# A third weight buffer, an earlier weight load and a rearranged head loop in a decode-attention gradient kernel

## The chip, the cores and the metric

The kernel runs on one core of a Trainium2 chip. The metric is device time in microseconds (us), the median over several runs. The profiled execution of each kernel is some 2 us shorter in its span than its timed run, so spans are compared with spans and timed runs with timed runs.

Engine names in the profile: PE is TensorE's matmuls, PEld its weight loads, DVE is VectorE, ACT is ScalarE, POOL is GpSimd, SP is SyncE. In this kernel SP issues nearly all loads and POOL issues nearly all stores. The order in which each engine runs its instructions is chosen by a scheduler in the framework and is fixed when the kernel is built. I call it the built order. It is not always the order of the source.

## The reference, cut to what matters

One decode step of a block, and all its gradients: layer norm, attention against a cache, and a gated MLP, both added to the input.

```python
# D=640, 32 heads, Dh=128, Sk=8192 cached positions, F=1728, all bf16
q  = (xn @ wq) per head;   p = softmax(q @ K^T * Dh**-0.5);   o = p @ V
y  = x + o @ wo + (silu(xn @ w1) * (xn @ w3)) @ w2
# returned: y, and the gradients by x, K, V, wq, wo, w1, w3, w2
```

There is one query row, so the gradients of a head's cache are outer products: `dV = P (x) do` and `dK = U (x) q`, where `do = wo . grad_out` for that head, `U = P * (V.do - sum(P * V.do))`. Each is as large as the cache itself: 2 MB for K and 2 MB for V per head. The kernel reads 151.67 MB and writes 151.34 MB.

## The kernel before

A K or V tile of 2 MB is loaded into one of ten slots, used by TensorE, overwritten in place with its gradient by DVE, and stored from the same slot. Only then is the slot free for the next load. Four heads form a *group*. They share a slice of `wq` and one of `wo` (640 KB each), which are loaded, used, overwritten with their gradients and stored in the same manner.

```python
wpool = ctx.enter_context(tc.tile_pool(name="wp", bufs=2))    # group weights
tpool = ctx.enter_context(tc.tile_pool(name="tp", bufs=5))    # "KT": transposed K/V pieces
junk  = consts.tile([P, D], BF16, name="junk")                # one tile for thrown-away output
...
def load_group(g):                       # SP queue
    wq_g = wpool.tile([P, NC, GW], BF16, name="wq_g", tag="wq_g")      # rows of 1024 bytes
    nc.sync.dma_start(wq_g[:], wq_v[:, :, g * GW:(g + 1) * GW])
    wo_g = wpool.tile([P, GH, D], BF16, name="wo_g", tag="wo_g")       # rows of 1280 bytes
    nc.sync.dma_start(wo_g[:], wo_v[:, g * GH:(g + 1) * GH, :])
...
def prep_group(g):
    ...                                  # wide q product, on TensorE, from wq_g
    for hh in range(GH):                 # "the wo product", on DVE
        nc.vector.scalar_tensor_tensor(junk[:], wo_g[:, hh, :], 1.0, g_bc[:], ALU.mult, ALU.mult,
                                       accum_out=do_c[:, hh:hh + 1])
    ...
def phase_b(h):
    ...                                  # sums over V and K on TensorE
    for lo in range(0, J, J // 2):
        outer(Vt, doh, P2, lo, lo + J // 2)          # DVE, dV over V
    nc.gpsimd.dma_start(dvc[h], Vt[:])
    free_slots.append(Vt); load_next()               # next K or V load, into a free slot
    for lo in range(0, J, J // 2):
        outer(Kt, qh, U2, lo, lo + J // 2)           # DVE, dK over K
    nc.gpsimd.dma_start(dkc[h], Kt[:])
    free_slots.append(Kt); load_next()
...
def finish_group(g):
    ...                                  # dwo over wo_g (4 DVE instructions), store
    for ci in range(NC):                 # "the wq pairs"
        nc.vector.scalar_tensor_tensor(junk[:, 0:GW], wq_g[:, ci, :], 1.0, dqb[:], ALU.mult, ALU.mult,
                                       accum_out=dxa[:, ci, g:g + 1])
        nc.vector.tensor_scalar(wq_g[:, ci, :], dqb[:], xn_col[:, ci:ci + 1], None, ALU.mult)
    nc.gpsimd.dma_start(dwq_v[:, :, g * GW:(g + 1) * GW], wq_g[:])
...
for h in range(H):
    g, hh = divmod(h, GH)
    if hh == 2 and g + 1 < NG:
        load_group(g + 1)
    if hh == 3 and g + 1 < NG:
        prep_group(g + 1)
    phase_b(h)
    if h == 1:
        mlp()
    if h + 1 < H:
        phase_k(h + 1)                   # K.q, softmax
        phase_v(h + 1)                   # V.do
    if hh == GH - 1:
        finish_group(g)
```

## Time and profile before

| | before |
|---|---|
| time, first three runs | 802.82 us (801.28 to 804.2) |
| span of the profiled run | 796.0 us |
| moved by DMA | 304.61 MB, mean 383 GB/s |
| TensorE busy | 76% |
| VectorE busy | 56% |
| VectorE waiting for a `wo` load | 119.2 us in 6 waits |

First the page of the kernel before: busy time by engine, then the span in 40 slices (each digit is a busy share in tenths), with the mean DMA rate of each slice below.

```profile
span 796.0 us, 25112 instructions
PE 601.1 (76%) x11271; PEld 553.2 (69%) x11271; DVE 444.3 (56%) x771; ACT 327.1 (41%) x652; POOL 53.1 (7%) x93
...
PE   3988880189989549992799819995599918999981
...
DMA  8999999996999998999899998999999998998656
GB/s 328 388 425 424 423 424 428 422 373 244 415 421 426 429 381 340 412 409 418 354 379 403 426 425 324 393 404 422 376 375 408 411 426 349 374 400 363 274 212 278
DMA packets 35182, 304.61 MB, mean 383 GB/s; under 512 B 2836, under 2 KB 14036, under 8 KB 18692
```

The DMA rate tops out at 420 to 430 GB/s, and the kernel reaches that in many slices. The Trainium skill ("DMA: Bandwidth & Descriptors", Specifications) names 435 GB/s as fabric ceiling, and the trace agrees to within a few per cent. But there are dips (244, 340, 354, 324, 349 GB/s) and a slow end (274, 212, 278). TensorE's row has holes (`01`, `54`, `27`, `81`), about one per group of four heads.

The waits of the kernel before tell what stands in those holes. The columns are what waited, for what, total us, number of waits, longest wait. The first fence is of the engines:

```profile
DVE junk L231 <- DMA wo_g<-in_A_wo_dram: 119.2, 6, 31.5
...
PEld L218 <- DMA wq_g<-in_A_wq_dram: 34.3, 1, 34.3
```

The second is of SP's queue, in the same kernel:

```profile
SPq L115 <- DMA out_dram<-kv: 556.8, 56, 21.5
...
SPq L103 <- DMA out_dram<-wo_g: 48.8, 6, 18.3
SPq L101 <- DMA out_dram<-wq_g: 11.6, 6, 3.2
```

Line 231 is the wo product. Six times DVE waits for the load of the next group's `wo`, 20 us on average. SP in turn waits for the store of the old `wo` gradient (48.8 us in all) before it can issue that load: with two buffers, the load of group g+1 goes into the buffer of group g-1.

One of the six, on the timeline of DVE before (start, duration, instruction, and in brackets the idle time ahead of it with what ended it):

```profile
454.80 0.22 DVE L291 TENSOR_REDUCE mrow<-sA 128x1 f32<-128x64 f32 x1
455.04 0.17 DVE L333 MEMSET hb<- 128x129 f32 x1
472.60 0.83 DVE L231 SCALAR_TENSOR_TENSOR junk<-wo_g,g_bc 128x640 bf16<-128x640 bf16 x1 [17.39 <-DMA wo_g<-in_A_wo_dram]
...
473.35 0.29 DVE L295 TENSOR_REDUCE negM<-sA 128x1 f32<-128x128 f32 x1
```

and on the timeline of SP before:

```profile
454.72 0.38 SPq L103 DMA_DIRECT2D wo_g<-in_A_wo_dram  x1
464.60 0.33 SPq L115 DMA_DIRECT2D kv<-in_A_k_cache_dram  x1
469.85 0.33 SPq L115 DMA_DIRECT2D kv<-in_A_v_cache_dram  x1
471.94 0.38 SPq L101 DMA_DIRECT2D wq_g<-in_A_wq_dram  x1
```

DVE has computed the row maximum of a head (`mrow`) at 455.02. The next step of that softmax, `negM`, comes at 473.35, behind the first wo product. DVE runs in order, so the softmax of a head that needs nothing of this `wo` stands still for 17.39 us.

What the stall does to the DMA engines is seen in the windows of the kernel before (stretch, its length, busy us and instruction count of PE, PEld, DVE, ACT and POOL, then TensorE's granted clock, DMA share, GB/s):

```profile
465.00:470.00 5.00, 0.00 (x0) 0.00 (x0) 0.00 (x0) 0.00 (x0) 0.00 (x0) 0.50 0.97 394
480.00:485.00 5.00, 4.70 (x119) 4.57 (x116) 5.00 (x4) 1.82 (x4) 0.30 (x1) 1.00 0.50 177
740.00:760.00 20.00, 18.74 (x386) 17.54 (x386) 12.36 (x13) 9.65 (x19) 1.09 (x2) 1.00 0.52 213
```

During the stall the DMA engines still have work (394 GB/s). The price comes 10 us later, when what is queued has been moved and no slot has come free (177 GB/s), and at the end of the span, where loads are over and only stores are left (213 GB/s). The granted clock also falls to 0.50 while TensorE stands still, and is 1.00 again at 480 us. The Trainium skill ("TensorE: Matmul & The Clock Gate", Part 1) says that an idle TensorE falls to half clock after a few us; the trace agrees: TensorE's last instruction before the stall ends at 456.8 us, and the clock is halved at 461.2.

### The profile page before, as it was taken

Reading aid. Unit: us, or ns where it says so; the run is one execution under the profiler, and the core shown is the slowest. Engines: PE = TensorE matmul, PEld = TensorE weight load, DVE = VectorE, ACT = ScalarE, POOL = GpSimd, SP = SyncE. Lnnn points to the kernel's source line nnn. Section 1 sums busy time; section 2 is a strip of 40 time slices with the busy share of each in tenths; the row PEclk is TensorE's granted clock in tenths of the full one; section 3 lists DMA queues with packets and bytes.
Section 4 is the critical chain, followed back from the end, with each engine's and each line's share of the span. In section 5 each row is a group of like instructions: output and inputs, shape, how many; then the busy total and the mean of one; then the engine's idle time right before and its main releaser. Section 6 shows DMA issues by size and latency. Waiting matters only on the chain. (4 is left out here: it accounts for less than half of the span.)

```text
span 796.0 us, 25112 instructions
## 1 busy us (share of the span) xinstructions
PE 601.1 (76%) x11271; PEld 553.2 (69%) x11271; DVE 444.3 (56%) x771; ACT 327.1 (41%) x652; POOL 53.1 (7%) x93
## 2 busy tenths in 40 slices
PE   3988880189989549992799819995599918999981
PEld 2877870088888438892788818895588818888871
DVE  4479463138646436572655715575465717558567
ACT  2621540055455214552355405553155514555540
POOL 0001000000000000000000100000000000001001
PEclk9998995589999869997899959999699978999996
DMA  8999999996999998999899998999999998998656
GB/s 328 388 425 424 423 424 428 422 373 244 415 421 426 429 381 340 412 409 418 354 379 403 426 425 324 393 404 422 376 375 408 411 426 349 374 400 363 274 212 278
DMA packets 35182, 304.61 MB, mean 383 GB/s; under 512 B 2836, under 2 KB 14036, under 8 KB 18692
## 3 DMA queue, kind: packets, MB, share of 16 engines
q1 hardware_dynamic: 21828, 151.35, 47.1%
q0 software_dynamic: 12960, 151.34, 45.8%
q8 instruction: 88, 1.44, 0.7%
q10 hardware_dynamic: 288, 0.33, 0.2%
q14 instruction: 18, 0.15, 0.0%
HBM read 151.67 MB, written 151.34 MB: 381 GB/s over the span
## 5 line engine op out<-in xcount | busy, mean ns | idle before, releaser
L270 ACT COPY KT<-pT 128x512 f32<-128x512 f32 x512 | 293.8, 588 | 202.9 <-PE pT L268 162.4
L268 PE MATMUL pT<-ident_f,kv 128*128 128x128 f32 x2048 | 334.8, 287 | 0.1
L268 PEld LDWEIGHTS pT<-ident_f,kv 128*128 128x128 f32 x2048 | 230.1, 145 | 0.7 <-issue 0.3
L279 PEld LDWEIGHTS <-KT 128*128 128x128 bf16 x4096 | 182.7, 99 | 26.1 <-ACT KT L270 18.7
L316 DVE TENSOR_TENSOR kv<-do_g,P 128x4096 bf16<-128x4096 bf16 x64 | 146.3, 2286 | 31.3 <-PE hb L339 31.3
L316 DVE TENSOR_TENSOR kv<-qs_g,U 128x4096 bf16<-128x4096 bf16 x64 | 144.2, 2284 | 0.4 <-PE hb L345 0.4
L279 PE MATMUL dA<-cz,KT 128*128 128x64 bf16 x2048 | 102.4, 196 | 3.9 <-ACT KT L270 2.2
L279 PE MATMUL sA<-cz,KT 128*128 128x64 bf16 x2048 | 100.5, 193 | 3.9 <-ACT KT L270 0.3
L231 DVE SCALAR_TENSOR_TENSOR junk<-wo_g,g_bc 128x640 bf16<-128x640 bf16 x32 | 26.1, 816 | 119.3 <-DMA wo_g<-in_A_wo_dram 119.2
L345 PEld LDWEIGHTS <-kv 128*128 128x128 bf16 x2048 | 67.9, 98 | 20.8 <-issue 20.7
L299 PE MATMUL sA<-rsum,ones_f 128*128 128x1 f32 x64 | 13.3, 276 | 90.6 <-ACT E L298 87.9
L345 PE MATMUL hb<-U,kv 128*128 128x64 bf16 x2048 | 69.2, 193 | 16.1 <-DVE U L342 11.1
L299 PEld LDWEIGHTS sA<-rsum,ones_f 128*128 128x128 f32 x64 | 10.5, 207 | 97.4 <-ACT E L298 97.4
L339 PE MATMUL hb<-P,kv 128*128 128x64 bf16 x2048 | 68.3, 192 | 0.3 <-issue 0.3
L339 PEld LDWEIGHTS <-kv 128*128 128x128 bf16 x2048 | 67.8, 98 | 0.5 <-issue 0.4
L336 DVE SCALAR_TENSOR_TENSOR junk<-dA,P 128x64 f32<-128x64 f32 x32 | 7.2, 224 | 94.8 <-PE dA L279 94.7
L349 POOL DMA_DIRECT2D out_dram<-kv x32 | 17.4, 542 | 488.8 <-DVE kv L316 488.8
L298 ACT ACTIVATE E<-sA,negM 128x64 f32<-128x64 f32 x32 | 10.2, 319 | 86.3 <-DVE negM L295 86.2
L218 PE MATMUL pT<-wq_g,xn_col_bf 128*128 128x512 bf16 x40 | 13.0, 441 | 38.5 <-DMA wq_g<-in_A_wq_dram 34.2
L357 ACT COPY od_g<-hb 128x2 f32<-128x2 f32 x32 | 5.1, 160 | 85.5 <-DVE kv L316 48.1
L218 PEld LDWEIGHTS <-xn_col_bf 128*128 128x128 bf16 x40 | 3.7, 106 | 41.8 <-DMA wq_g<-in_A_wq_dram 34.3
L302 DVE RECIPROCAL rZ<-sA 128x1 f32<-128x1 f32 x32 | 5.4, 168 | 40.5 <-PE sA L299 40.5
(131 smaller groups left out, 344.1 us busy)
## 6 DMA issues: line engine op xcount, KB each, us to landing
out_dram<-kv POOLq DMA_DIRECT2D x64, 2048.0 KB, 13.8
kv<-in_A_k_cache_dram SPq DMA_DIRECT2D x32, 2048.0 KB, 13.0
kv<-in_A_v_cache_dram SPq DMA_DIRECT2D x32, 2048.0 KB, 14.6
wq_g<-in_A_wq_dram SPq DMA_DIRECT2D x8, 640.0 KB, 12.2
wo_g<-in_A_wo_dram SPq DMA_DIRECT2D x8, 640.0 KB, 16.9
out_dram<-wo_g POOLq DMA_DIRECT2D x8, 640.0 KB, 12.2
out_dram<-wq_g POOLq DMA_DIRECT2D x8, 640.0 KB, 15.6
kv<-in_B_w_dram SPq DMA_DIRECT2D x2, 1728.0 KB, 19.2
```

Of the source, the lines that this page charges most:

```text
L218: nc.tensor.matmul(ps_q[:, 0:GW], lhsT=xn_col_bf[:, ci:ci + 1].to_broadcast([P, P]), rhs=wq_g[:, ci, :], start=(ci == 0), stop=(ci == NC - 1))
L231: nc.vector.scalar_tensor_tensor(junk[:], wo_g[:, hh, :], 1.0, g_bc[:], ALU.mult, ALU.mult, accum_out=do_c[:, hh:hh + 1])
L268: nc.tensor.transpose(pT[:, k * P:(k + 1) * P], W3[:, 4 * c + k, :], ident_f[:])
L270: nc.scalar.copy(KT[:].rearrange("p k w -> p (k w)"), pT[:])
L279: nc.tensor.matmul(out_[:, 0:J], lhsT=KTb[:, k, par, :], rhs=cz[:, par, a, J - 2 - 2 * i:ZW - 2 * i], start=(i == 0 and par == 0), stop=(p ...
L298: nc.scalar.activation(E[:], sA[:, 0:J], ACTF.Exp, bias=negM[:], scale=1.0, accum_out=rsum[:])
L299: nc.tensor.matmul(sA[:, J + P:J + P + 1], lhsT=ones_f[:], rhs=rsum[:], start=False, stop=True, skip_group_check=True)
L316: nc.vector.tensor_tensor(dst[:, lo * DH:hi * DH].rearrange("p (j a b) -> p j a b", a=DH // 2, b=2), vec.rearrange("p (a b) -> p a b", b=2 ...
L336: nc.vector.scalar_tensor_tensor(junk2[:], dA[:, 0:J], 1.0, P2[:, :, 0], ALU.mult, ALU.mult, accum_out=rdot[:])
L339: nc.tensor.matmul(hb[:, 0:RW], lhsT=V3[:, j, :], rhs=P2[:, j, 0:1].to_broadcast([P, RW]), start=False, stop=(j == J - 1), skip_group_chec ...
L345: nc.tensor.matmul(hb[:, RW:2 * RW], lhsT=K3[:, j, :], rhs=U2[:, j, 0:1].to_broadcast([P, RW]), start=False, stop=(j == J - 1), skip_group ...
L349: nc.gpsimd.dma_start(dvc[h], Vt[:])
```

## The change

The intent, as given: three weight-group buffers, so that each group is loaded one head ahead of its first use without waiting for a store; and the softmax chain of head h+1 placed between the outer products of head h. To make room in memory for the third buffer, several tiles are removed or lent. The core of the diff:

```diff
-    wpool = ctx.enter_context(tc.tile_pool(name="wp", bufs=2))
-    tpool = ctx.enter_context(tc.tile_pool(name="tp", bufs=5))
+    wpool = ctx.enter_context(tc.tile_pool(name="wp", bufs=3))
+    tpool = ctx.enter_context(tc.tile_pool(name="tp", bufs=4))
 ...
 def load_next():
         kind, h = pending.pop(0)
+        if kind == "K" and h % GH == GH - 1 and h // GH + 1 < NG:
+            load_group(h // GH + 1)
 ...
-    junk = consts.tile([P, D], BF16, name="junk")
 ...
 def prep_group(g):
-        ps_q = pst()                                  # wide q product and its copy: gone
-        ...
+        junk = t_tile()[:, 0:D]                       # a KT tile, taken anew each time
         for hh in range(GH):
-            nc.vector.scalar_tensor_tensor(junk[:], wo_g[:, hh, :], 1.0, g_bc[:], ALU.mult, ALU.mult,
+            nc.vector.scalar_tensor_tensor(junk, wo_g[:, hh, :], 1.0, g_bc[:], ALU.mult, ALU.mult,
                                            accum_out=do_c[:, hh:hh + 1])
-        ps_o = pst()                                  # wide do broadcast and its copy: gone
-        ...
+    def rows(h):                                      # per head: q and do rows, two 128x128 products, one copy
+        ...
 ...
 def finish_group(g):
-        dqb = small.tile([P, GW], BF16, name="dqb", bufs=1)
+        dqb = t_tile()[:, 0:GW]
         for ci in range(NC):
-            nc.vector.scalar_tensor_tensor(junk[:, 0:GW], wq_g[:, ci, :], 1.0, dqb[:], ALU.mult, ALU.mult,
+            nc.vector.scalar_tensor_tensor(wq_g[:, ci, :], wq_g[:, ci, :], 1.0, dqb, ALU.mult, ALU.mult,
                                            accum_out=dxa[:, ci, g:g + 1])
 ...
 for h in range(H):
         g, hh = divmod(h, GH)
-        if hh == 2 and g + 1 < NG:
-            load_group(g + 1)
         if hh == GH - 1 and g + 1 < NG:
             prep_group(g + 1)
-        phase_b(h)
+        sums(h)
+        outer_v(h, 0, J // 2)
+        outer_v(h, J // 2, J)
+        store("V", h)
         if h == 1:
             mlp()
         if h + 1 < H:
-            phase_k(h + 1)
-            phase_v(h + 1)
+            rows(h + 1)
+            dots_k(h + 1)
+        outer_k(h, 0, J // 2)
+        if h + 1 < H:
+            probs(h + 1)
+        outer_k(h, J // 2, J)
+        store("K", h)
+        if h + 1 < H:
+            dots_v(h + 1)
```

More of the change, by code (lines that the diff above doesn't have):

```diff
@@ L90 @@
     RW = 64
-    x_bc_bf = consts.tile([P, D], BF16, name="x_bc_bf")
-    nc.scalar.dma_start(x_bc_bf[:], A_x.rearrange("a b d -> (a b d)").partition_broadcast(P))
+    x_kt = tpool.tile([P, 4, P], F32, name="x_kt", tag="KT")
+    x_bc_bf = x_kt[:].rearrange("p k w -> p (k w)").bitcast(BF16)[:, 0:D]
+    nc.scalar.dma_start(x_bc_bf, A_x.rearrange("a b d -> (a b d)").partition_broadcast(P))
     g_bc = consts.tile([P, D], BF16, name="g_bc")
@@ L150 @@
     nc.vector.tensor_copy(ident_bf[:], ident_f[:])
-    ones_f = consts.tile([P, P], F32, name="ones_f")
-    nc.vector.memset(ones_f[:], 1.0)
-    negones_f = consts.tile([P, P], F32, name="negones_f")
-    nc.vector.memset(negones_f[:], -1.0)
+    pm_one = consts.tile([P, 2], F32, name="pm_one")
+    nc.vector.memset(pm_one[:, 0:1], 1.0)
+    nc.vector.memset(pm_one[:, 1:2], -1.0)
+    ones_b = pm_one[:, 0:1].to_broadcast([P, P])
+    negones_b = pm_one[:, 1:2].to_broadcast([P, P])
     one_bf = consts.tile([P, 1], BF16, name="one_bf")
@@ L190, in pst @@
         return ps_t.tile([P, 512], F32, name="pT", tag="pT")
-    junk = consts.tile([P, D], BF16, name="junk")
     msum = consts.tile([P, 1], F32, name="msum")
-    nc.vector.tensor_reduce(msum[:], x_bc_bf[:], AX.X, ALU.add)
+    nc.vector.tensor_reduce(msum[:], x_bc_bf, AX.X, ALU.add)
     nc.vector.tensor_scalar(negmean[:], msum[:], -1.0 / D, None, ALU.mult)
     sumsq = consts.tile([P, 1], F32, name="sumsq")
-    nc.vector.scalar_tensor_tensor(junk[:], x_bc_bf[:], negmean[:], x_bc_bf[:], ALU.add, ALU.mult,
+    nc.vector.scalar_tensor_tensor(t_tile()[:, 0:D], x_bc_bf, negmean[:], x_bc_bf, ALU.add, ALU.mult,
                                    accum_out=sumsq[:])
@@ L215, in prep_group @@
         wq_g, wo_g = G_["wq"], G_["wo"]
-        ps_q = pst()
-        for ci in range(NC):
-            nc.tensor.matmul(ps_q[:, 0:GW], lhsT=xn_col_bf[:, ci:ci + 1].to_broadcast([P, P]), rhs=wq_g[:, ci, :],
-                             start=(ci == 0), stop=(ci == NC - 1))
-        qs_g = wpool.tile([P, GH, DH], BF16, name="qs_g", tag="qs_g")
-        nc.scalar.activation(qs_g[:].rearrange("p h d -> p (h d)"), ps_q[:, 0:GW], ACTF.Copy, scale=scale)
         cb = wpool.tile([P, 2, GH], BF16, name="cb", tag="cb")
@@ L228, in prep_group @@
         nc.scalar.activation(cb[:, 0, :], ps_c[:, 0:GH], ACTF.Copy, scale=scale)
+        junk = t_tile()[:, 0:D]
         do_c = wpool.tile([P, GH], F32, name="do_c", tag="do_c")
         for hh in range(GH):
-            nc.vector.scalar_tensor_tensor(junk[:], wo_g[:, hh, :], 1.0, g_bc[:], ALU.mult, ALU.mult,
+            nc.vector.scalar_tensor_tensor(junk, wo_g[:, hh, :], 1.0, g_bc[:], ALU.mult, ALU.mult,
                                            accum_out=do_c[:, hh:hh + 1])
         nc.vector.tensor_copy(cb[:, 1, :], do_c[:])
-        ps_o = pst()
-        for hh in range(GH):
-            nc.tensor.matmul(ps_o[:, hh * DH:(hh + 1) * DH], lhsT=cb[:, 1, hh:hh + 1].to_broadcast([P, P]),
-                             rhs=ident_bf[:], start=True, stop=True)
-        do_g = wpool.tile([P, GH, DH], BF16, name="do_g", tag="do_g")
-        nc.scalar.copy(do_g[:].rearrange("p h d -> p (h d)"), ps_o[:, 0:GW])
         ps_m = pst()
@@ L248, in prep_group @@
         od_g = wpool.tile([P, GH, 2], F32, name="od_g", tag="od_g")
-        G_.update(qs=qs_g, cm=cm_g, do=do_g, od=od_g)
+        G_.update(cb=cb, cm=cm_g, od=od_g)
     hd = {}
@@ L281, in dots, with dots_k @@
                                          start=(i == 0 and par == 0), stop=(par == 1), skip_group_check=True)
-    def phase_k(h):
+    def rows(h):
         g, hh = divmod(h, GH)
-        cm = grp[g]["cm"]
+        cb, cm = grp[g]["cb"], grp[g]["cm"]
         cz = cz_tiles[h % 2]
         nc.vector.tensor_copy(cz[:, :, :, J - 2:J], cm[:, :, :, hh, :])
+        ps_r = pst()
+        for a in range(2):
+            nc.tensor.matmul(ps_r[:, a * DH:(a + 1) * DH], lhsT=cb[:, a, hh:hh + 1].to_broadcast([P, P]),
+                             rhs=ident_bf[:], start=True, stop=True)
+        qd = small.tile([P, 2, DH], BF16, name="qd")
+        nc.scalar.copy(qd[:].rearrange("p a d -> p (a d)"), ps_r[:, 0:2 * DH])
+        hd[h] = dict(cz=cz, qd=qd)
+    def dots_k(h):
+        S_ = hd[h]
         sA = ps_s.tile([P, 512], F32, name="sA", tag="sA")
-        dots(kv_tiles[("K", h)], sA, cz, 0)
+        dots(kv_tiles[("K", h)], sA, S_["cz"], 0)
         mrow = small.tile([P, 1], F32, name="mrow")
@@ L298, in phase_k, with probs, dots_v @@
         nc.scalar.activation(E[:], sA[:, 0:J], ACTF.Exp, bias=negM[:], scale=1.0, accum_out=rsum[:])
-        nc.tensor.matmul(sA[:, J + P:J + P + 1], lhsT=ones_f[:], rhs=rsum[:],
+        nc.tensor.matmul(sA[:, J + P:J + P + 1], lhsT=ones_b, rhs=rsum[:],
                          start=False, stop=True, skip_group_check=True)
+        S_.update(sA=sA, E=E)
+    def probs(h):
+        S_ = hd[h]
         rZ = small.tile([P, 1], F32, name="rZ")
-        nc.vector.reciprocal(rZ[:], sA[:, J + P:J + P + 1])
+        nc.vector.reciprocal(rZ[:], S_["sA"][:, J + P:J + P + 1])
         P2 = small.tile([P, J, 2], BF16, name="P2")
-        nc.vector.tensor_scalar(P2[:], E[:].unsqueeze(2).to_broadcast([P, J, 2]), rZ[:], None, ALU.mult)
-        hd[h] = dict(P2=P2)
-    def phase_v(h):
-        g, hh = divmod(h, GH)
-        cz = cz_tiles[h % 2]
+        nc.vector.tensor_scalar(P2[:], S_["E"][:].unsqueeze(2).to_broadcast([P, J, 2]), rZ[:], None, ALU.mult)
+        S_["P2"] = P2
+    def dots_v(h):
+        S_ = hd[h]
         dA = ps_d.tile([P, 512], F32, name="dA", tag="dA")
-        dots(kv_tiles[("V", h)], dA, cz, 1)
-        hd[h]["dA"] = dA
+        dots(kv_tiles[("V", h)], dA, S_["cz"], 1)
+        S_["dA"] = dA
     def outer(dst, vec, pair, lo, hi):
@@ L319, in outer, with sums @@
             pair[:, lo:hi, :].unsqueeze(2).to_broadcast([P, n, DH // 2, 2]), ALU.mult)
-    def phase_b(h):
+    def sums(h):
         g, hh = divmod(h, GH)
-        G_ = grp[g]
-        qh = G_["qs"][:, hh, :]
-        doh = G_["do"][:, hh, :]
-        Kt = kv_tiles.pop(("K", h))
-        Vt = kv_tiles.pop(("V", h))
-        S_ = hd.pop(h)
+        S_ = hd[h]
         P2, dA = S_["P2"], S_["dA"]
-        V3 = Vt[:].rearrange("p (j d) -> p j d", d=DH)
-        K3 = Kt[:].rearrange("p (j d) -> p j d", d=DH)
+        V3 = kv_tiles[("V", h)][:].rearrange("p (j d) -> p j d", d=DH)
+        K3 = kv_tiles[("K", h)][:].rearrange("p (j d) -> p j d", d=DH)
@@ L332, in phase_b @@
         hb = ps_h.tile([P, 2 * RW + 1], F32, name="hb", tag="hb")
         nc.vector.memset(hb[:], 0.0)
-        junk2 = small.tile([P, J], F32, name="junk2", bufs=1)
+        U2 = small.tile([P, J, 2], BF16, name="U2")
         rdot = small.tile([P, 1], F32, name="rdot")
-        nc.vector.scalar_tensor_tensor(junk2[:], dA[:, 0:J], 1.0, P2[:, :, 0], ALU.mult, ALU.mult, accum_out=rdot[:])
-        nc.tensor.matmul(hb[:, 2 * RW:2 * RW + 1], lhsT=negones_f[:], rhs=rdot[:], start=False, stop=True, skip_group_check=True)
+        nc.vector.scalar_tensor_tensor(U2[:, :, 0], dA[:, 0:J], 1.0, P2[:, :, 0], ALU.mult, ALU.mult, accum_out=rdot[:])
@@ L338, in phase_b @@
+        nc.tensor.matmul(hb[:, 2 * RW:2 * RW + 1], lhsT=negones_b, rhs=rdot[:], start=False, stop=True,
+                         skip_group_check=True)
         for j in range(J):
-            nc.tensor.matmul(hb[:, 0:RW], lhsT=V3[:, j, :], rhs=P2[:, j, 0:1].to_broadcast([P, RW]), start=False, stop=(j == J - 1),
-                             skip_group_check=True)
-        U2 = small.tile([P, J, 2], BF16, name="U2")
-        nc.vector.scalar_tensor_tensor(U2[:], dA[:, 0:J].unsqueeze(2).to_broadcast([P, J, 2]), hb[:, 2 * RW:2 * RW + 1], P2[:],
-                                       ALU.add, ALU.mult)
@@ L344, in phase_b @@
-        for j in range(J):
-            nc.tensor.matmul(hb[:, RW:2 * RW], lhsT=K3[:, j, :], rhs=U2[:, j, 0:1].to_broadcast([P, RW]), start=False, stop=(j == J - 1),
-                             skip_group_check=True)
-        for lo in range(0, J, J // 2):
-            outer(Vt, doh, P2, lo, lo + J // 2)
-        nc.gpsimd.dma_start(dvc[h], Vt[:])
-        free_slots.append(Vt)
-        load_next()
-        for lo in range(0, J, J // 2):
-            outer(Kt, qh, U2, lo, lo + J // 2)
-        nc.gpsimd.dma_start(dkc[h], Kt[:])
@@ L355, in phase_b @@
-        free_slots.append(Kt)
-        load_next()
-        nc.scalar.copy(G_["od"][:, hh, :], hb[:, RW - 1:RW + 1])
+            nc.tensor.matmul(hb[:, 0:RW], lhsT=V3[:, j, :], rhs=P2[:, j, 0:1].to_broadcast([P, RW]), start=False,
+                             stop=(j == J - 1), skip_group_check=True)
+        nc.vector.scalar_tensor_tensor(U2[:], dA[:, 0:J].unsqueeze(2).to_broadcast([P, J, 2]),
+                                       hb[:, 2 * RW:2 * RW + 1], P2[:], ALU.add, ALU.mult)
+        for j in range(J):
+            nc.tensor.matmul(hb[:, RW:2 * RW], lhsT=K3[:, j, :], rhs=U2[:, j, 0:1].to_broadcast([P, RW]), start=False,
+                             stop=(j == J - 1), skip_group_check=True)
@@ L359, with outer_v, outer_k, store @@
+        nc.scalar.copy(grp[g]["od"][:, hh, :], hb[:, RW - 1:RW + 1])
+        S_["U2"] = U2
+    def outer_v(h, lo, hi):
+        outer(kv_tiles[("V", h)], hd[h]["qd"][:, 1, :], hd[h]["P2"], lo, hi)
+    def outer_k(h, lo, hi):
+        outer(kv_tiles[("K", h)], hd[h]["qd"][:, 0, :], hd[h]["U2"], lo, hi)
+    def store(kind, h):
+        t = kv_tiles.pop((kind, h))
+        nc.gpsimd.dma_start((dkc if kind == "K" else dvc)[h], t[:])
+        free_slots.append(t)
+        load_next()
     dxa = consts.tile([P, NC, NG], F32, name="dxa")
@@ L370, in finish_group @@
                              rhs=ident_bf[:], start=True, stop=True)
-        dqb = small.tile([P, GW], BF16, name="dqb", bufs=1)
-        nc.scalar.copy(dqb[:], ps_b[:, 0:GW])
+        dqb = t_tile()[:, 0:GW]
+        nc.scalar.copy(dqb, ps_b[:, 0:GW])
         for hh in range(GH):
@@ L380, in finish_group @@
         for ci in range(NC):
-            nc.vector.scalar_tensor_tensor(junk[:, 0:GW], wq_g[:, ci, :], 1.0, dqb[:], ALU.mult, ALU.mult,
+            nc.vector.scalar_tensor_tensor(wq_g[:, ci, :], wq_g[:, ci, :], 1.0, dqb, ALU.mult, ALU.mult,
                                            accum_out=dxa[:, ci, g:g + 1])
-            nc.vector.tensor_scalar(wq_g[:, ci, :], dqb[:], xn_col[:, ci:ci + 1], None, ALU.mult)
+            nc.vector.tensor_scalar(wq_g[:, ci, :], dqb, xn_col[:, ci:ci + 1], None, ALU.mult)
         nc.gpsimd.dma_start(dwq_v[:, :, g * GW:(g + 1) * GW], wq_g[:])
@@ L503 @@
     prep_group(0)
-    phase_k(0)
-    phase_v(0)
+    rows(0)
+    dots_k(0)
+    probs(0)
+    dots_v(0)
     for h in range(H):
         g, hh = divmod(h, GH)
-        if hh == 2 and g + 1 < NG:
-            load_group(g + 1)
-        if hh == 3 and g + 1 < NG:
+        if hh == GH - 1 and g + 1 < NG:
             prep_group(g + 1)
-        phase_b(h)
+        sums(h)
+        outer_v(h, 0, J // 2)
+        outer_v(h, J // 2, J)
+        store("V", h)
         if h == 1:
@@ L515 @@
         if h + 1 < H:
-            phase_k(h + 1)
-            phase_v(h + 1)
+            rows(h + 1)
[7 more added lines that the diff above has]
+            dots_v(h + 1)
+        hd.pop(h)
         if hh == GH - 1:
@@ L532 @@
     ps_f = pst()
-    nc.tensor.matmul(ps_f[:, 0:2], lhsT=ones_f[:], rhs=st[:], start=True, stop=True)
+    nc.tensor.matmul(ps_f[:, 0:2], lhsT=ones_b, rhs=st[:], start=True, stop=True)
     nst = consts.tile([P, 2], F32, name="nst")
```

## The prediction

> **What bounds the kernel now.** The DMA engines, and a stall at each group boundary. The page: span 796 us, 304.6 MB moved, mean 383 GB/s. Where slots turn freely (35 to 165 and 200 to 270 us in the windows view) the mean is about 420 GB/s at a DMA share of 1.0. The Trainium skill ("DMA: Bandwidth & Descriptors", Specifications) gives 435 GB/s as fabric ceiling; the trace agrees to a few per cent. At 420 the traffic takes 725 us.
>
> TensorE is not the long-run limit. Unstalled, head follows head every 17.7 us (outer products at 484.3 and 502.0 us); a head's K and V traffic is 8.39 MB, 20 us at 420 GB/s, about 21.5 with its share of the projection weights.
>
> But TensorE stands still 15 to 35 us per group boundary: in 455 to 475 us nearly unused, and DVE ends a 17.4-us wait on the wo load. The waits view sums 119 us in six such waits. The SP queue view shows why: the load waits for the store of an earlier group from the two-buffer pool (wo 48.8 us over six, wq 11.6), among cache loads. DMA meanwhile goes on at 420 GB/s; the price comes later: a dip after each restart (480 to 485 us: 177 GB/s; 180 to 185: nothing), and a tail. The last V load is issued at 705 us with four heads still to do: 740 to 780 us run at 213 to 225 GB/s.
>
> **Removed.** A third buffer takes the store out of the load's way. In the built order groups 1 and 2 are queued just before K3 and K7, later ones two heads earlier still. The boundary stalls go. TensorE loses the wide q product (40 of 0.38 us, 15 us) and gains two small products a head.
>
> **Added.** KT buffers fall from 5 to 4, also lent as scratch to group work: 0 to 5 us.
>
> **Moved.** The scheduler undoes nearly all of the softmax interleaving: in most heads max, negated max, reciprocal and P still stand after both K outer products of the preceding head. 0 to 2 us.
>
> **How much counts.** Not the 119 us of waits: DMA covers most. The DMA idle time counts: by windows (1 minus share, times length) about 28 us of dips, 25 of tail. Estimate: loads end when all but about 9.5 MB has moved: 293 MB at 420 GB/s plus 4 us start, 702 us; from V landing to the end about 30 us (as after 766 us in before): 732; weights in 1-KB rows and remaining dips about 14: span 746. Timed runs were 0.9% over the span: 753 us.
>
> Predicted **753 us**, range 738 to 785. Faster by over 2%: 0.93; within 2%: 0.06; slower: 0.01.
>
> **What would show it.** (1) No DVE wait on wo at boundaries beyond a few us. (2) SP waits on weight stores near zero. (3) Mean rate above 400 GB/s, share about 1.0 from 20 to 700 us. (4) TensorE waits become short, on K and V loads; heads 20 to 22 us apart. (5) Last V load issued no earlier than before, tail under 35 us.
>
> **What would make it wrong.** K's sums of a head stand behind the next head's K transposes on TensorE, so slots are held while waiting for loads: DMA could dip in the steady state. Or scratch in the KT pool stalls TensorE at boundaries, or the MLP, with fewer buffers, drains the DMA queue.

## The result, and the profile after

| | before | after |
|---|---|---|
| time, four runs each | 802.05 us (800.57 to 804.2) | 749.69 us (748.93 to 751.46) |
| ratio after / before | | 0.9348 (0.9318 to 0.9378) |
| span | 796.0 | 748.2 |
| mean DMA rate | 383 GB/s | 407 GB/s |
| mean granted TensorE clock | 0.901 | 0.927 |

A ratio is the mean time of one kernel's fast runs over the mean of the other's of the same rounds, so it is not quite the ratio of the medians quoted. The brackets are 95% intervals.

The page of the kernel after:

```profile
span 748.2 us, 25141 instructions
PE 594.4 (79%) x11263; PEld 550.9 (74%) x11263; DVE 445.3 (60%) x771; ACT 329.8 (44%) x668; POOL 53.6 (7%) x93
...
PE   2988798993889999429986999829989499998961
...
DMA  8999999999999999999999999999998999999976
GB/s 324 387 420 423 421 422 429 427 414 430 423 420 425 424 428 422 425 429 427 390 362 411 424 428 422 379 424 430 427 417 316 423 426 430 425 427 426 425 294 259
```

The engines do the same work in nearly the same busy time. The DMA row is full nearly throughout. What is left of dips are slices of 362, 379 and 316 GB/s, and the end.

The waits of the kernel after, for the engines:

```profile
PE pT L260 <- DMA kv<-in_A_k_cache_dram: 70.7, 7, 24.5
...
DVE KT L229 <- PE dA L271: 15.4, 7, 2.2
```

and for SP's queue:

```profile
SPq L118 <- DMA out_dram<-kv: 195.1, 21, 23.6
...
SPq L102 <- DMA out_dram<-wq_g: 14.3, 2, 7.2
...
SPq L104 <- DMA out_dram<-wo_g: 12.0, 2, 6.0
```

The wo product (now line 229) waits for no load any more, only for TensorE, 2.2 us at most. SP waits 26.3 us for weight stores in place of 60.4. In their place a new wait has come: TensorE waits seven times for a K load, 24.5 us at the longest. That one, on the timeline of TensorE after:

```profile
306.87 0.27 PE L282 MATMUL pT<-ident_bf,cb 128*128 128x128 bf16 x2
331.61 2.79 PE L260 MATMUL pT<-ident_f,kv 128*128 128x128 f32 x12 [24.46 <-DMA kv<-in_A_k_cache_dram]
```

The next such episode starts in SP's queue after:

```profile
331.56 0.38 SPq L104 DMA_DIRECT2D wo_g<-in_A_wo_dram  x1
336.43 0.38 SPq L102 DMA_DIRECT2D wq_g<-in_A_wq_dram  x1
341.32 45.67 SPq L118 DMA_DIRECT2D kv<-in_A_k_cache_dram  x1
387.16 2.95 SPq L118 DMA_DIRECT2D kv<-in_A_v_cache_dram  x1
```

The issue of one K load took 45.67 us, where others take 0.33. The next longest were 42.74, 37.10, 24.33, 21.90, 19.91 and 19.69 us. All seven are the K load right behind a pair of weight loads; the eighth (14.16 us) is the next K load after one of them. And the windows of the kernel after:

```profile
315.00:325.00 10.00, 0.00 (x0) 0.00 (x0) 0.00 (x0) 0.00 (x0) 0.58 (x1) 0.50 1.02 431
385.00:390.00 5.00, 3.46 (x107) 3.33 (x104) 4.96 (x7) 0.37 (x1) 0.00 (x0) 1.00 0.73 263
```

TensorE stands still for all of 315 to 325 us, but now the DMA engines move 431 GB/s meanwhile. A dip to 263 GB/s comes at the end of the second episode. The longest issue does not go with the longest pause: the next wait of TensorE for a K load, at 412.61 us, was 6.8 us.

### Where the time went, counted in DMA time

Both kernels move the same bytes. So the difference of their spans must be a difference of DMA rate, and the question is only where. I took the windows view in 5-us steps and added up (1 - rate / 425 GB/s) x 5 us over each stage. A step above 425 GB/s counts as nothing lost.

| stage (us) | before | scratch edits alone | after | wide packets | GpSimd queue |
|---|---|---|---|---|---|
| 0 to 20 | 4.7 | 4.6 | 4.5 | 3.6 | 4.7 |
| 20 to 120 | 2.8 | 2.7 | 2.9 | 2.7 | 3.1 |
| 120 to 700 | 47.8 | 23.1 | 15.6 | 5.2 | 7.3 |
| 700 to end | 28.2 | 25.5 | 13.1 | 20.7 | 19.3 |
| sum | 83.4 | 56.1 | 36.2 | 32.2 | 34.5 |
| span | 796.0 | 768.6 | 748.2 | 743.7 | 747.3 |

("Scratch edits alone", "wide packets" and "GpSimd queue" are experiments below; sums are of unrounded values.) From before to after the sum falls by 47.2 us, and the span by 47.8. With equal bytes the two must nearly agree, so this is arithmetic and no evidence; what the table shows is the place. Of this, 32 us came from the dips between 120 and 700 us and 15 from the end. Nothing came from the first 120 us.

### The profile page after: what moved, and what is told of

It reads as the page before. It is cut to its first block, busy times and chain, and to the rows that moved or that the text cites. A ratio compares the mean times of both kernels' runs of the same rounds, so it can differ in the third digit from the quotient of the medians.

```text
span 748.2 us, 25141 instructions
## 1 busy us (share of the span) xinstructions
PE 594.4 (79%) x11263; PEld 550.9 (74%) x11263; DVE 445.3 (60%) x771; ACT 329.8 (44%) x668; POOL 53.6 (7%) x93
## 5 line engine op out<-in xcount | busy, mean ns | idle before, releaser
L260 PE MATMUL pT<-ident_f,kv 128*128 128x128 f32 x2048 | 334.7, 287 | 75.3 <-DMA kv<-in_A_k_cache_dram 70.7
L321 DVE TENSOR_TENSOR kv<-qd,U 128x4096 bf16<-128x4096 bf16 x64 | 144.3, 2285 | 48.5 <-PE hb L345 48.5
L321 DVE TENSOR_TENSOR kv<-qd,P 128x4096 bf16<-128x4096 bf16 x64 | 145.7, 2286 | 42.1 <-PE hb L340 42.1
L345 PEld LDWEIGHTS <-kv 128*128 128x128 bf16 x2048 | 68.6, 98 | 13.2 <-issue 13.0
L345 PE MATMUL hb<-U,kv 128*128 128x64 bf16 x2048 | 69.5, 193 | 9.3 <-DVE U L342 6.4
L358 POOL DMA_DIRECT2D out_dram<-kv x64 | 34.9, 546 | 567.8 <-DVE kv L321 309.1
L336 DVE SCALAR_TENSOR_TENSOR U<-dA,P 128x64 bf16<-128x64 f32 x32 | 7.4, 231 | 77.0 <-PE dA L271 77.0
L285 ACT CAST qd<-pT 128x256 bf16<-128x256 f32 x32 | 12.0, 375 | 54.4 <-PE pT L282 54.4
L229 DVE SCALAR_TENSOR_TENSOR KT<-wo_g,g_bc 128x640 bf16<-128x640 bf16 x32 | 26.4, 824 | 15.9 <-PE dA L271 15.4
L293 DVE TENSOR_REDUCE mrow<-sA 128x1 f32<-128x64 f32 x32 | 6.5, 203 | 33.3 <-PE sA L271 33.2
L384 DVE SCALAR_TENSOR_TENSOR wq_g<-wq_g,KT 128x512 bf16<-128x512 bf16 x40 | 26.2, 686 | 0.0
L297 DVE TENSOR_REDUCE negM<-sA 128x1 f32<-128x128 f32 x32 | 9.3, 291 | 14.5 <-PE sA L294 14.5
L301 PEld LDWEIGHTS sA<-rsum,pm_one 128*128 128x128 f32 x64 | 9.5, 187 | 11.2 <-ACT E L300 11.2
```

Of the source, the lines that this page charges most:

```text
L229: nc.vector.scalar_tensor_tensor(junk, wo_g[:, hh, :], 1.0, g_bc[:], ALU.mult, ALU.mult, accum_out=do_c[:, hh:hh + 1])
L260: nc.tensor.transpose(pT[:, k * P:(k + 1) * P], W3[:, 4 * c + k, :], ident_f[:])
L285: nc.scalar.copy(qd[:].rearrange("p a d -> p (a d)"), ps_r[:, 0:2 * DH])
L297: nc.vector.tensor_reduce(negM[:], sA[:, J:J + P], AX.X, ALU.max, negate=True)
L301: nc.tensor.matmul(sA[:, J + P:J + P + 1], lhsT=ones_b, rhs=rsum[:], start=False, stop=True, skip_group_check=True)
L321: nc.vector.tensor_tensor(dst[:, lo * DH:hi * DH].rearrange("p (j a b) -> p j a b", a=DH // 2, b=2), vec.rearrange("p (a b) -> p a b", b=2 ...
```

## The experiments

The explanation that the change itself suggests, and that the prediction gave, is this: the third buffer takes the weight store out of the load's way, and so the stalls at group boundaries go. Rivals: the early load, with any number of buffers; the loop order; the per-head rows in place of the wide q product; and the edits made only to save memory.

### The loop order, undone

```diff
+        sums(h); outer_v(h, 0, J // 2); outer_v(h, J // 2, J); store("V", h)
+        outer_k(h, 0, J // 2); outer_k(h, J // 2, J); store("K", h)
+        if h == 1: mlp()
+        if h + 1 < H:
+            rows(h + 1); dots_k(h + 1); probs(h + 1); dots_v(h + 1)
```

> The changed kernel with the loop order of before: both V outer products, both K outer products, both stores, then rows, K dots, softmax and V dots of the next head. Weight buffers and load position stay changed. Theory B (third buffer): the interleaving is worth nothing, so 748 to 753 us, within 0.5% of the changed kernel (749.7). Theory I (interleaving): a good part of the 52 us is lost, 765 us or more.

Measured: 750.52 us, ratio 0.9359 (0.9327 to 0.939); the change has 0.9348. The rearranged loop is worth 0.8 us in the medians, less than the intervals can tell from nothing. In the built order of the changed kernel the interleaving survives in one head of each group only: in the other three both K outer products stand ahead of the next head's maximum, as before.

### Two buffers, or the load in its old place, or both

```diff
# e2: two buffers
-    wpool = ctx.enter_context(tc.tile_pool(name="wp", bufs=3))
+    wpool = ctx.enter_context(tc.tile_pool(name="wp", bufs=2))
# e3: the load in its old place
-        if kind == "K" and h % GH == GH - 1 and h // GH + 1 < NG:
-            load_group(h // GH + 1)
+        if hh == 2 and g + 1 < NG:          # in the head loop
+            load_group(g + 1)
# e4: both
```

> The changed kernel with two weight-group buffers instead of three; the early position of the load and the interleaving stay. Theory B: the load again waits for the store of an earlier group, at the head of the in-order load queue; TensorE stalls return, 780 to 805 us, SP waits on weight stores of 40 us or more in all. Theory I: 765 us or less.

> The changed kernel with three buffers, but the group load back at its old place in the loop (head 2 of the group before). In the built order only the load of group 1 then comes late (after V6 instead of before K3); later ones are hoisted to nearly the same places, since a buffer is free. Theory B: one long stall of TensorE at the first boundary (some 30 us near 120 to 160 us), most of it covered by DMA: 750 to 760 us. Theory P (position of the load is what matters, not the buffer): 780 us or more.

> Both undone: two buffers and the old load position; what is left of the change is the interleaving, the row products per head and four KT buffers. Theory B: nearly the time of before, 785 to 805 us. Theory I: 775 us or less.

Measured, with the ratio to the kernel before:

| | load at the old place | load one head ahead |
|---|---|---|
| two buffers | 769.89 us, 0.96 (0.9551 to 0.9648) | 761.15 us, 0.9474 (0.9424 to 0.9524) |
| three buffers | 755.68 us, 0.9425 (0.9394 to 0.9456) | 749.69 us, 0.9348 (0.9318 to 0.9378) |

Theory B missed twice here: it expected 780 to 805 us for two buffers and 785 to 805 for both undone. Yet with two buffers SP's waits for weight stores did return, as it expected:

```profile
SPq L104 <- DMA out_dram<-wo_g: 46.3, 6, 15.7
SPq L102 <- DMA out_dram<-wq_g: 42.8, 6, 7.5
```

That is 89.1 us, more than the 60.4 of the kernel before, in a kernel that is 42 us faster (761.15 against 803.59). So these waits do not set the time by themselves.

Buffers and load together take 20 us (769.89 to 749.69). The buffer is worth 11 to 14 us, the early load 6 to 9. In the kernel with three buffers and the old load place, one boundary still shows the old stall, a 31.4-us wait of the wo product on its load and a 34.1-us wait on `wq`: that of group 1, whose load in the built order comes late, behind V6.

The surprise is the upper left cell. With neither the buffer nor the early load, and with a loop order that the run above had shown to be worth nothing, the kernel was still 4% faster than before. Some 32 of the 52 us come from something else. What else had changed was the row products, one KT buffer fewer, and the edits to save memory.

### The scratch edits, alone, on the kernel before

```diff
# f3: both of these, and nothing else, on the kernel before
+        junk_ = t_tile()[:, 0:D]
-            nc.vector.scalar_tensor_tensor(junk[:], wo_g[:, hh, :], 1.0, g_bc[:], ALU.mult, ALU.mult,
+            nc.vector.scalar_tensor_tensor(junk_, wo_g[:, hh, :], 1.0, g_bc[:], ALU.mult, ALU.mult,   # f3b
-            nc.vector.scalar_tensor_tensor(junk[:, 0:GW], wq_g[:, ci, :], 1.0, dqb[:], ALU.mult, ALU.mult,
+            nc.vector.scalar_tensor_tensor(wq_g[:, ci, :], wq_g[:, ci, :], 1.0, dqb[:], ALU.mult, ALU.mult,   # f3a
```

> The kernel before with both scratch edits and nothing else: two weight buffers, the old load position, the old loop, the wide q product, five KT buffers. If the scratch edits explain why undoing the buffers and the load position gave 770 us and not 802, this gives 766 to 774 us too. If the row products, the interleaving or the slimmer group work do, it stays above 785 us.

> The kernel before with one edit: the elementwise product of the wq gradient is written back over wq instead of into the shared scratch tile. In the built order this alone lets the group's five wq pairs run before the outer products, so the wq store is queued with the wo store, and the next wq load with the wo load. The wo product of the next group stays where it was, two heads early in VectorE's in-order stream. Theory D (that early product blocks VectorE until wo lands): little changes, 790 to 802 us, VectorE still waits 80 us or more on wo. Theory W (the late wq store and the split loads are what costs): 770 to 780 us.

> The kernel before with one edit: the throw-away output of the wo product goes into a KT buffer instead of the shared scratch tile. In the built order this moves the wo product from head 4g+1 to head 4g+3, its place in the program; the wq pairs stay spread between the outer products. Theory D: the wait on wo goes (except at the first group), 770 to 785 us with two weight buffers still. Theory W: 795 to 803 us.

Measured, with the kernel before at 804.47 us:

| | time | ratio to before |
|---|---|---|
| f3a: wq pairs in place | 801.82 us | 0.9971 (0.9914 to 1.0027) |
| f3b: wo product into a KT tile | 782.59 us | 0.974 (0.9694 to 0.9786) |
| f3: both | 770.33 us | 0.9586 (0.9541 to 0.963) |

Two edits that were made to save memory take 34 us by themselves, with two buffers, the old load place, the old loop, the wide q product and five KT buffers. That is 34 us of the 52 us, and it is what the upper left cell above has (770.33 against 769.89), so what else that kernel had changed (the row products, the loop order, one KT buffer fewer) adds up to nothing that can be seen. That single effects cancel is not excluded. One edit alone is worth nothing, the other 22 us, and the two together 34: they help each other.

What changed is the built order. With the thrown-away output in another tile, the scheduler put the same instructions in another order. This is DVE's built order over one group, from the finishing of the old group to the use of the next `wo` (wo4: gradient of `wo`; dx and wq: the wq pairs; dc: the wo product for the next group; OV, OK: outer products; each `|` starts a head):

```
before  rdot wo4 dx OV wq dx U2 wq dx OV wq dx OK wq dx OK wq | mrow dc negM dc rZ dc P dc rdot OV U2 OV OK2 | ... | ...
f3a     rdot wo4 dx2 wq2 dx2 wq2 dx U2 wq OV2 OK2             | mrow dc negM dc rZ dc P dc rdot OV U2 OV OK2 | ... | ...
f3b     rdot wo4 dx OV wq dx U2 wq dx OV wq dx OK wq dx OK wq | mrow negM rZ P rdot OV U2 OV OK2 | ... | mrow negM rZ P dc2 rdot dc2 OV ...
f3      rdot wo4 dx2 wq2 dx2 wq2 dx U2 wq OV2 OK2             | mrow negM rZ P rdot OV U2 OV OK2 | ... | mrow negM rZ P dc2 rdot dc2 OV ...
```

The f3b edit moves the wo product by two heads, from the second head of a group to the fourth, where the source has it, and out of the middle of a softmax. The f3a edit finishes the wq pairs before the outer products, so that the store of the old `wq` is issued sooner and SP can load the next `wq` sooner: in the same group the `wq` load is issued 17.2 us after the `wo` load before, 17.4 in f3b, but 6.4 in f3a and 7.6 in f3, with no K or V load between. The waits follow. Of f3a:

```profile
DVE junk L231 <- DMA wo_g<-in_A_wo_dram: 121.1, 6, 28.7
```

of f3b:

```profile
PEld L218 <- DMA wq_g<-in_A_wq_dram: 96.1, 6, 33.7
...
DVE KT L232 <- DMA wo_g<-in_A_wo_dram: 31.0, 1, 31.0
```

and of f3:

```profile
PEld L218 <- DMA wq_g<-in_A_wq_dram: 83.0, 5, 35.6
...
DVE KT L232 <- DMA wo_g<-in_A_wo_dram: 58.4, 5, 32.9
```

In f3a the wo product still waits six times, as before, and nothing is gained. In f3b those waits fall to one, and TensorE's waits on the late `wq` load take their place. In f3 both loads come close together. Its waits do not vanish (83.0 and 58.4 us, and they overlap), but the dips between 120 and 700 us fall from 47.8 to 23.1 us (27.8 in f3b). Why the scheduler chooses these orders was not looked into. That the order is what counts, and nothing else about the tiles, is inferred: VectorE is as busy as before (446.2 us in f3, 444.3 before), so the edits save no work, but no run forced the order alone with two buffers.

### Is the place of the wo product what costs, even with three buffers?

The opposite test: the changed kernel, with the wo product and the rest of the group's preparation put two heads early again. It is not quite the place of before: in this built order the product stands behind the softmax of that head (after P), not inside it, and the wq pairs stay ahead of the outer products.

```diff
-        if hh == GH - 1 and g + 1 < NG:
+        if hh == 1 and g + 1 < NG:
             prep_group(g + 1)
```

> The changed kernel (three buffers, early load) with the next group's preparation moved two heads earlier in the program, so that the wo product stands on VectorE at head 4g+1, where the scheduler had put it before the change. Theory S (the early product costs only when the weights are late; a third buffer makes them early, so its place no longer matters): 748 to 757 us, VectorE waits on wo of under 40 us in all, and those at the first two boundaries, where the load is queued late. Theory D (the place of the product is what costs, whatever the buffers): 765 us or more.

Measured: 753.52 us, ratio 0.9391 (0.9366 to 0.9417), 4 us over the change. The wo product waits on its load at a single boundary:

```profile
DVE KT L229 <- DMA wo_g<-in_A_wo_dram: 19.4, 1, 19.4
```

So the two causes are not independent, and the gain cannot be split in one way only. With two buffers, moving the wo product and the wq pairs is worth 34 us. With three buffers and the early load, the weights are there in time at all boundaries but one, and the early head for the wo product costs only 4 us. The prediction's mechanism may thus be worth nearly the whole gain too, where the scratch edits are missing, but that is not shown: no kernel with the buffers and without both scratch edits was run. (The changed kernel with a scratch tile of its own for the wo product does not build: it does not fit into memory.) Counted in the order of the runs, the scratch edits did 34 of the 52 us without the third buffer, and the buffer with its early load added 20 (sums from different rounds, hence 54).

### What are TensorE's remaining pauses? Wide packets

After the change TensorE still stands still for 10 to 25 us at four of the boundaries, waiting for a K load. A K or V tile travels in packets of 16 KB, `wq` in packets of 1024 bytes and `wo` of 1280. The packets of the trace after that ended between 284.5 and 294.5 us of the span: 231 of 16 KB for stores (615 ns each), 6 of 16 KB for K and V loads, and 306 of 1024 or 1280 bytes for weight loads (53 ns each), 427 GB/s in all. Between 339.5 and 344.5 us no store packet was moved, and 127 load packets of 16 KB were. So while stores and weight loads are both queued, a DMA engine gives a store 16 KB and a load about 1 KB, roughly in turn, and stores get nearly all of the rate. The Trainium skill ("DMA: Bandwidth & Descriptors", Queues, rings and completion order) says that each DMA engine goes round-robin between its queues, a packet at a time; the counts agree roughly, with packets as the trace records them (312 load packets to 231 store packets, where strict turns would give as many of each), and show what it means when packets differ 16-fold. A group's weights are 72 small packets per DMA engine (40 of `wq`, 32 of `wo`). Estimate from the durations above: 72 x (0.615 + 0.053) us = 48 us, if a store packet stands between every two. The longest K issue behind a weights load was 45.67 us.

To test it, load the weights as contiguous memory, 5120 bytes to a partition. The values are then wrong (three outputs are off, by about 1.4 of their size); the bytes moved and the instructions of the compute engines are the same.

```diff
+    wq_flat = A_wq.rearrange("a b -> (a b)").rearrange("(g p x) -> g p x", p=P, x=NC * GW)
-        nc.sync.dma_start(wq_g[:], wq_v[:, :, g * GW:(g + 1) * GW])
+        nc.sync.dma_start(wq_g[:].rearrange("p c n -> p (c n)"), wq_flat[g])
# wo the same way
```

> The changed kernel, but each group's weights are loaded from contiguous memory, 5120 bytes per partition, instead of rows of 1024 and 1280 bytes: the same bytes, about a fifth of the packets. The gradients and outputs that use these weights are wrong on purpose. Theory A (in the changed kernel the small load packets take turns one for one with 16-KB store packets on each DMA engine, so the 72 small packets per engine of a group hold back the K load behind them by about 45 us, which makes the remaining TensorE pauses of 10 to 28 us and the DMA dips near 390 and 570 us): the longest K-load issue falls from 46 us to under 20 us, TensorE pauses over 10 us mostly go, 735 to 745 us. Theory T (loads are late only because all bandwidth is used; packet size does not matter): issue times and pauses stay, 747 to 752 us.

Measured: 745.4 us (745.03 to 745.87), ratio 0.9298 (0.9274 to 0.9322). After the first 30 us no K or V load took over 10 us to issue; in the change eight took 14 to 46. The longest wait of TensorE for K fell to 10.7 us, and the sum of these waits from 70.7 to 57.5:

```profile
PE pT L262 <- DMA kv<-in_A_k_cache_dram: 57.5, 10, 10.7
```

The dips between 120 and 700 us fell from 15.6 to 5.2 us of DMA time. So the size of the weight packets, and with it their number, is what makes the long pauses; theory A's 735 to 745 us was missed by 0.4. But the kernel gained only 4 us, 0.5%, with intervals that touch: the end took 20.7 us of DMA time in place of 13.1. The last V load landed at 695.3 us in place of 708.8, and VectorE's last instruction came 15.7 us sooner than in the change. First with wide packets, then in the kernel after:

```profile
724.70 0.28 DVE L559 CAST fin_bf<-pT 10x128 bf16<-10x128 f32 x1 [0.56 <-PE pT L557]
```

```profile
740.38 0.28 DVE L557 CAST fin_bf<-pT 10x128 bf16<-10x128 f32 x1 [0.55 <-PE pT L555]
```

But the span went on for 18.7 us after it (to 743.7), against 7.5 in the change. The DMA engines were still storing then, at a share of 0.06:

```profile
730.00:740.00 10.00, 0.00 (x0) 0.00 (x0) 0.00 (x0) 0.00 (x0) 0.00 (x0) 0.50 0.06 27
```

A share of 0.06 of 16 engines is about one engine (0.06 x 16 = 1.0, an estimate): the packets of the last stores follow one another at some 611 ns each, as if one DMA engine had fallen behind the other fifteen. The trace does not name the engine of a packet, and why one should lag was not looked into. So the wide packets did make the computing end 16 us sooner, and the drain of the last stores took 11 of these back.

### Other ways around the pauses, with right results

```diff
# e6: weights of groups 1 to 7 through ScalarE's queue
+        eng = nc.sync if g == 0 else nc.scalar
# e10: nine pieces, each ahead of another K or V load, every SP load pinned behind the one before
+        for gk in pieces.get((kind, h), []):
+            load_piece(*gk)
# e14: through GpSimd's queue, pinned behind the K store two heads after the old group is finished
+        nxt = {0: 1, 2: 2}.get(h, g + 2 if hh == 1 and h > GH else NG)
+        if nxt < NG:
+            load_group(nxt)
```

> The changed kernel with the group weights (from the second group on) loaded through ScalarE's DMA queue instead of SyncE's, so K and V loads no longer stand behind them. Results stay right. Theory A: K loads are issued in under 5 us each, 738 to 748 us; the risk is that ScalarE itself waits at these loads for the store of an earlier group and holds up the transposes. Theory T: 747 to 752 us.

> The changed kernel with each group's weights loaded in nine pieces (five of wq, four of wo), one or two in front of each K or V load, in an order pinned in the SyncE queue. The same packets, spread. Results stay right. Theory A: each K or V load is held back by 5 to 10 us instead of one by 45 us; longest issue under 20 us, TensorE pauses over 10 us mostly go, 738 to 747 us. Theory T: 747 to 752 us.

> The changed kernel with the weights loaded through GpSimd's DMA queue, behind the store of K two heads after the group finished, so that the buffer is free by then and K and V loads never stand behind weights. Results stay right. If this queue moves a partition's rows in larger packets[...], theory A expects what the wide packets gave, 743 to 748 us, and no K-load issue over 10 us after the first 40 us. If the packets stay small, or the stores behind them are held back, or GpSimd waits, 750 to 760 us.

Measured:

| | time | ratio to before | TensorE's longest wait on K |
|---|---|---|---|
| the change | 749.69 us | 0.9348 (0.9318 to 0.9378) | 24.5 us |
| e6, ScalarE's queue | 762.08 us | 0.9506 (0.9483 to 0.9529) | none among the largest waits |
| e10, nine pieces | 754.8 us | 0.9434 (0.9403 to 0.9464) | 7.5 us |
| e14, GpSimd's queue | 749.37 us | 0.9344 (0.9323 to 0.9365) | 8.3 us |

In e6 the stall moved to ScalarE, which now waits for the weight stores in its own instruction stream, ahead of its copies:

```profile
ACT od_g L348 <- DMA out_dram<-wo_g: 74.0, 5, 19.0
```

The Trainium skill ("DMA: Bandwidth & Descriptors", Issuing engines are not separate DMA queues) says that another issuing engine saves only its sequencer's time. Here the kernel became 12 us slower, with ScalarE waiting 102.8 us for weight stores (74.0 for `wo`, 28.8 for `wq`).

In e10 the pauses are short and no K or V load takes over 4 us to issue, yet the kernel is 5 us slower than the change. In its profiled run, the fastest of the six (752.33 us), the dips took 10.8 us of DMA time and the end 18.2, against 15.6 and 13.1 in the change, and VectorE ended at 743.4 us, later than in the change (740.7). Why stays open.

In e14 the weight loads stand in the same queue as the stores. The trace records them as packets of 4096 bytes (`wq`) and 5120 bytes (`wo`), the sizes of the stores of the same gradients. No K load took over 10 us to issue after the first 40 us, and the dips fell to 7.3 us of DMA time. GpSimd paid for it, harmlessly:

```profile
POOL wq_g L104 <- DMA out_dram<-wq_g: 133.1, 5, 31.6
```

The time is that of the change, for the same reason as with wide packets: VectorE ends at 727.5 us, 13 us sooner than in the change, but from 735 to 745 us the DMA share is 0.06 again, and the span ends at 747.3. What the dips gave back the end took (19.3 us in place of 13.1). Two kernels without the long pauses gained 0 and 4 us. That does not make the pauses free: without them the computing ended 13 and 16 us sooner, and the last stores hid most of it. The 738 to 748, 738 to 747 and 743 to 748 us that theory A expected of e6, e10 and e14 were all missed.

A changed kernel with five KT buffers could not be tried: it does not build, as it does not fit into memory. No version with right results was clearly faster than the change.

## Why the prediction was right or wrong

The time was right: 753 us predicted, 749.69 measured, well inside 738 to 785, and faster by more than 2%. How it came out so close is in part luck.

- **"The DMA engines, and a stall at each group boundary": right.** The dips and the end, which the prediction put at 28 and 25 us, are what shrank. In the table's DMA time, which is counted by rate and not by busy share, they were 47.8 and 28.2, and fell to 15.6 and 13.1.
- **The estimate of the time: right in the sum, off in its terms.** Loads were to end at 702 us plus about 14 for small rows and remaining dips, 716 in all; the last one landed at 708.8. From there to the end 30 us were predicted, and 39.4 measured. And 0.9%, 7 us, were added from span to timed run, where 2.2 us were measured (748.2 to 750.44); the 0.9% had compared the profiled run of before with the median of other, slower runs (798.28 against 802.82 us). The errors, 7 us too much, 9 too little and 5 too much, nearly cancel.
- **"A third buffer takes the store out of the load's way. ... The boundary stalls go": only part of the cause.** Without the third buffer and the early load, 34 of the 52 us were already gained (770.33 us), by two scratch edits that moved the wo product out of the softmax and the wq pairs ahead of the outer products in the built order. The prediction had looked at the built order for the weight loads and the softmax, but not for the wo product and the wq pairs. It booked those edits as a possible cost. And the stalls did not all go: TensorE still pauses 10 to 25 us at four boundaries, now for K loads behind small weight packets.
- **"Added: 0 to 5 us" for fewer KT buffers and lent scratch: no cost seen** (769.89 us with four buffers, against 770.33 with five), and the gain from the lending was missed.
- **"Moved: 0 to 2 us" for the softmax interleaving: right,** 0.8 us.
- **(1) No wait on `wo` beyond a few us: right.** None is listed.
- **(2) Waits on weight stores near zero: too strong.** 26.3 us, from 60.4.
- **(3) Mean rate above 400 GB/s: right,** 407. The share is near 1.0, apart from dips as low as 172 GB/s (share 0.46, from 560 to 565 us).
- **(4) TensorE waits short, heads 20 to 22 us apart: wrong.** Waits on K reached 24.5 us. The V stores of four heads in a row are issued at 273.85, 291.96, 315.11 and 354.85 us: 18, 23 and 40 us apart. What the prediction named under "What would make it wrong" did happen here: the sums over K stood on TensorE behind the next head's K transposes, so VectorE held the K slot while that load was late (`hb` L345 is the sum over K):

```profile
336.97 2.29 DVE L321 TENSOR_TENSOR kv<-qd,U 128x4096 bf16<-128x4096 bf16 x1 [22.16 <-PE hb L345]
```

- **(5) Last V load issued no earlier than before: wrong,** 660.60 us against 705.23 (counted back from the end, 87.6 us against 90.8). "Tail under 35 us", counted from the landing of that load: wrong, 39.4 (76.4 before).

What failed is the step from "SP waits for the store of a two-buffer pool" to "so the pool is the cause". The wait on the store was real, but it set the time only together with the place where its consumer stood: with two buffers, moving the consumer took 34 of the 52 us, and the two-buffer kernel that waited longest for stores (89.1 us) was 42 us faster than before. The sum came out right because the stalls were priced by the DMA time they lost, whatever ended them, and because the errors in its terms cancelled.

## What to carry to other kernels

Before crediting a change's headline, run the change without it: here the edits that only made room were worth 34 us of 52, because a scheduler put the same instructions in another order. Where an in-order engine waits for a load, look at what stands behind the waiting instruction, and ask whether it could stand later, before buying another buffer. And when a pause is removed and the time stays, look at the end of the span before calling the pause free: here two ways of removing the last pauses let the computing end 13 and 16 us sooner and gained 0 and 4 us, because the last stores came out of the DMA engines at a sixteenth of the rate.

## What the Trainium skill lacked or had wrong

- "DMA: Bandwidth & Descriptors", Bandwidth, says in its comparison of three figures, without a condition, that between HBM and on-chip memory the HBM side binds at about 358 GB/s; a note above it keeps this for two cores that stream at once. One core, with loads and stores together, moved 420 to 430 GB/s for hundreds of us; the page's fabric ceiling of 435, and its own 425 GB/s for a transfer of 16 MB, are the figures that fit.
- "DMA: Bandwidth & Descriptors", Queues, rings and completion order, gives the round-robin by packet, but not its consequence for queues of unequal packets: with 16-KB stores queued, weight loads in rows of 1 to 1.3 KB got 306 packets to 231 of stores in 10 us, and behind one group of 1.3 MB the issue of a K load took up to 45.67 us.
- "DMA: Bandwidth & Descriptors", Issuing engines are not separate DMA queues, calls the issue time usually small against the transfer itself. Behind such weight loads the issue of one 2-MB load took 45.67 us on SP, where 0.33 is usual. That the issuing engine stands there because its queue is full is my reading; no run shows it, and I found no page that gives a depth for this queue.
- "DMA: Bandwidth & Descriptors", SWDGE vs HWDGE vs iDMA, prefers GpSimd packets of at most 4096 bytes, but does not say that the same copy travels in other packets through another issuing engine. Here the `wq` rows of 1024 bytes were 1024-byte packets through SP and 4096-byte packets through GpSimd, which agrees with that figure; `wo` had packets of 1280 and 5120 bytes, and a K or V tile 16384 on both, which do not.
